# Cached-attention decode: one softmax per head, K scored beside the previous head's V, all loads through one ring

## The chip, the cores and the metric

The kernel runs on one core of a Trainium2 chip. The metric is the device time of one execution in microseconds; the medians below are of several executions of the same program. The runs of one round share a chip, but the rounds used three different chips, so runs of different rounds are compared by their ratio to the kernel before, which ran in every round. The engines are PE (TensorE matmul, with its weight loads, PEld, beside it), DVE (VectorE), ACT (ScalarE), POOL (GpSimd) and SP (SyncE, which here only issues DMA).

## The reference

One decode step: attention of one query over a cache of 65536 keys in each of 32 heads, a small SwiGLU feed-forward on the same input, and a gate that mixes both. K and V are 512 MiB each in bf16; everything else is about 14 MB. So 1087.64 MB must be read once, and nothing large is written.

```python
# x: [1, 1, 512]; k_cache, v_cache: [1, 32, 65536, 128]; all bf16
q = (x @ wq).reshape(1, 1, 32, 128).transpose(0, 2, 1, 3)
scores = einsum("bhqd,bhkd->bhqk", q, k_cache) * 128 ** -0.5
o = einsum("bhqk,bhkd->bhqd", softmax(scores), v_cache)
a = o.transpose(0, 2, 1, 3).reshape(1, 1, 4096) @ wo
b = (silu(x @ w_gate) * (x @ w_up)) @ w_down
g = sigmoid((x * gate_w).sum(-1, keepdims=True))
out = g * a + (1 - g) * b
```

## The kernel before

The keys are cut into 512 chunks of 4096 (16 per head), 32 blocks of 128 keys each. Of the 32 blocks of a chunk, 16 are transposed on PE and scored there; the other 16 are scored on DVE, by a product and a sum. Each chunk has its own softmax: the maximum over the chunk, which needs an all-reduce over the partitions, an exponential, and a sum. The chunks of a head are rescaled to a common maximum at the very end. The parts that matter, with cuts marked:

```python
# GpSimd: for every chunk, an all-reduce and then a scaling
for g in range(NGC):                                   # NGC = 512
    pool.wait_ge(s_mx, g + 1)
    nc.gpsimd.partition_all_reduce(amxt[:, g:g + 1], mxs[:, g % 4:g % 4 + 1],
                                   P, RMAX).then_inc(s_ar, 1)                    # L255
    pool.wait_ge(s_ar, g + 1)
    nc.gpsimd.tensor_scalar_mul(nbias[:, g % 4:g % 4 + 1], amxt[:, g:g + 1],
                                -SCALE).then_inc(s_nb, 1)                        # L258
# ScalarE
for i in range(NGC + 2):
    ...                                # half of the K^T copies, L277
    g = i - 2
    if g >= 0:
        act.wait_ge(s_nb, g + 1)
        nc.scalar.activation(pcol[:, g % 2, :], psS[:, g % SCORE_BANKS, 0:RB], ACT.Exp,
                             bias=nbias[:, g % 4:g % 4 + 1], scale=SCALE,
                             accum_out=rsum[:, g:g + 1]).then_inc(expdone, 1)    # L283
# VectorE
for c in range(NGC):
    ...                                # the other half of the K^T copies, L342
    g = c - 2
    if g >= 0:
        dve.wait_ge(qkdone, g + 1)
        dve.wait_ge(qkd, g + 2)
        nc.vector.reduce_max(mxs[:, g % 4:g % 4 + 1], psS[:, g % SCORE_BANKS, 0:RB], AX_X) # L348
    ...
    if c >= SCORE_BANKS:               # SCORE_BANKS = 3
        dve.wait_ge(expdone, c - SCORE_BANKS + 1)
    nc.vector.tensor_tensor(prod3, kblocks(c, TB, RB), qb3, ALU.mult)            # L366
    dve.wait_ge(s_tt, c + 1)
    nc.vector.reduce_sum(psS[:, c % SCORE_BANKS, TB:RB], prod3, AX_X)            # L368
# TensorE: scores (L468), transposes (L477) and value matmuls (L489) of one chunk each, in turn
```

Of the kernel before, what the change touches and what calls it, by code (L numbers as in the profile page):

```python
# [5 lines left out]
P = 128  # L6
CK = 4096
RB = CK // 128
TB = 16
TD = RB - TB  # L10
HTB = TB // 2
NS = 6
SCORE_BANKS = 3
PV_LAG = 3
PRODMODE = "bcast_f32"

ALU = mybir.AluOpType
ACT = mybir.ActivationFunctionType
BF16 = mybir.dt.bfloat16
# [6 lines left out]
def bass_gated_mix__mha_block_cached__swiglu_ffn__decode_kernel(  # L26
# [16 lines left out]
    assert Dh == 128 and D % 128 == 0 and F % 128 == 0 and S % (2 * CK) == 0  # L43
    Dc = D // 128
    FC = F // 128
    NCH = S // CK
    NGC = H * NCH
    NIT = NGC // 2
    SCALE = float(Dh) ** -0.5
    QT_COL0 = 64  # L50
    assert NGC <= 512

    with ExitStack() as ctx:
# [9 lines left out]
        psT = psum("psT", [P, 2 * TB, 128], BF16)  # L63
        psS = psum("psS", [P, SCORE_BANKS, 512], F32)
# [6 lines left out]
        bT = sb("bT", [P, 8], F32)  # L71
        gbc = sb("gbc", [P, 4], F32)
        sc = sb("scal", [P, 16], F32)
        qTb = sb("qTb", [P, max(H, 16)], BF16)
        xTb = sb("xTb", [P, 16], BF16)
        hbuf = sb("hbuf", [P, 3, 16], F32)
        guT = sb("guT", [P, 16], BF16)
        pcol = sb("pcol", [P, 2, RB], BF16)
        mxs = sb("mxs", [P, 4], F32)
        amxt = sb("amxt", [P, NGC], F32)  # L80
        nbias = sb("nbias", [P, 4], F32)
        rsum = sb("rsum", [P, max(NGC, D)], F32)
        Mt = sb("Mt", [P, max(H, 8)], F32)
        oh = sb("oh", [P, max(H, 8)], F32)
        lp = sb("lp", [P, max(H, 8)], F32)
        Lt = sb("Lt", [P, max(H, 8)], F32)
        oTn = sb("oTn", [P, max(H, 16)], BF16)
        finT = sb("finT", [P, 8], BF16)
        fin = sb("finrow", [P, 128], BF16)
        GQ = 4 if H % 4 == 0 else (2 if H % 2 == 0 else 1)  # L90
        NGQ = H // GQ
        diag = sb("diag", [P, 2, GQ * 128], BF16)
        ring = sb("ring", [P, NS, 2 * CK], BF16)

        s_x = sem("s_x")
        s_w1 = sem("s_w1")
        s_wq = sem("s_wq")
        s_wo = sem("s_wo")
        rs = [sem(f"rs{i}") for i in range(NS)]
        s_id0 = sem("s_id0")  # L100
        s_ident = sem("s_ident")
        s_ones = sem("s_ones")
        s_xT = sem("s_xT")
        s_xTb = sem("s_xTb")
        s_z = sem("s_z")
        s_e1 = sem("s_e1")
        s_dch = sem("s_dch")
        s_h = sem("s_h")
        s_sig = sem("s_sig")
        s_gu = sem("s_gu")  # L110
        s_q = sem("s_q")
        s_qTb = sem("s_qTb")
        s_b = sem("s_b")
        s_pro_dve = sem("s_pro_dve")
        s_diag = sem("s_diag")
        s_qbm = sem("s_qbm")
        s_qbc = sem("s_qbc")
        tdone = sem("tdone")
        qkdone = sem("qkdone")
        qkd = sem("qkd")  # L120
        ktd = sem("ktd")
        kta = sem("kta")
        pvdone = sem("pvdone")
        s_mx = sem("s_mx")
        s_ar = sem("s_ar")
        s_nb = sem("s_nb")
        expdone = sem("expdone")
        s_M = sem("s_M")
        s_ew = sem("s_ew")
        s_oh = sem("s_oh")  # L130
        s_L = sem("s_L")
        s_otn = sem("s_otn")
        s_a = sem("s_a")
        s_fin = sem("s_fin")
        s_tt = sem("s_tt")
        s_qrep = sem("s_qrep")
        s_gbc = sem("s_gbc")
        s_tr = sem("s_tr")
        s_fin2 = sem("s_fin2")
        s_out = sem("s_out")  # L140

        xr_dram = A_x.rearrange("a b d -> (a b) d")
        out_dram = out.rearrange("a b (c p) -> (a b c) p", p=P)
        gw_dram = gate_w.rearrange("(a d) -> a d", a=1)
        wq_dram = A_wq.rearrange("(c p) n -> p c n", p=P)

# [5 lines left out]
        VLAG = 1  # L152
        ring_order = []
        for j in range(NIT):
            ring_order.append(("k", j))
            if j >= VLAG:
                ring_order.append(("v", j - VLAG))
        for j in range(max(0, NIT - VLAG), NIT):
            ring_order.append(("v", j))
        slotK = {}  # L160
        fillK = {}
        slotV = {}
        fillV = {}
        for i, (kind, j) in enumerate(ring_order):
            if kind == "k":
                slotK[j] = i % NS
                fillK[j] = i // NS + 1
            else:
                slotV[j] = i % NS
                fillV[j] = i // NS + 1  # L170

        def kv_src(kind, j):
            h = (2 * j) // NCH
            cc = (2 * j) % NCH
            src = A_k_cache if kind == "k" else A_v_cache
            return src[0, h, cc * CK:(cc + 2) * CK, :].rearrange("(p r) d -> p (r d)", p=P)

        def kblock(c, r):
            slot = slotK[c // 2]
            rr = (c % 2) * RB + r  # L180
            return ring[:, slot, rr * 128:(rr + 1) * 128]

        def kblocks(c, r0, r1):
            slot = slotK[c // 2]
            rr0 = (c % 2) * RB + r0
            rr1 = (c % 2) * RB + r1
            return ring[:, slot, rr0 * 128:rr1 * 128].rearrange("p (a b) -> p a b", b=128)

        def vblock(c, r):
            slot = slotV[c // 2]  # L190
            rr = (c % 2) * RB + r
            return ring[:, slot, rr * 128:(rr + 1) * 128]

        dve_chain = [0]
        omg_cnt = [0]

        with ExitStack() as phaseW:
            base_w = nc.sbuf_base
            wq_t = phaseW.enter_context(nc.sbuf_tensor("wq_t", [P, Dc, H * Dh], BF16))
            wq_ap = wq_t[:]  # L200
            w_end = nc.sbuf_base
        with ExitStack() as phaseM:
            KT = phaseM.enter_context(nc.sbuf_tensor("KT", [P, 3 * TB, 128], BF16))
            qbc = phaseM.enter_context(nc.sbuf_tensor("qbc", [P, H, 128], BF16))
            prod = phaseM.enter_context(nc.sbuf_tensor("prod", [P, TD * 128],
                                                       BF16 if PRODMODE == "qrep_bf16" else F32))
            if PRODMODE == "qrep_bf16":
                qrep = phaseM.enter_context(nc.sbuf_tensor("qrep", [P, TD * 128], BF16))
            if nc.sbuf_base < w_end:
                padm = phaseM.enter_context(nc.sbuf_tensor("padm", [P, (w_end - nc.sbuf_base + 64) // 2], BF16))  # L210
            with ExitStack() as phaseA:
                wg_t = phaseA.enter_context(nc.sbuf_tensor("wg_t", [P, Dc, F], BF16))
                wu_t = phaseA.enter_context(nc.sbuf_tensor("wu_t", [P, Dc, F], BF16))
                wd_t = phaseA.enter_context(nc.sbuf_tensor("wd_t", [P, FC, D], BF16))
                wg_ap = wg_t[:]
                wu_ap = wu_t[:]
                wd_ap = wd_t[:]
                a_end = nc.sbuf_base
            phaseB = ExitStack()
            wo_t = phaseB.enter_context(nc.sbuf_tensor("wo_t", [P, H, D], BF16))  # L220
            wo_ap = wo_t[:]
            if nc.sbuf_base < a_end:
                padb = phaseB.enter_context(nc.sbuf_tensor("padb", [P, (a_end - nc.sbuf_base + 64) // 2], BF16))

            block = phaseB.enter_context(nc.Block())

            @block.sync
            def _(sp):
                sp.dma_start(xrow[0:1, :], xr_dram).then_inc(s_x, 16)
                sp.dma_start(gwrow[0:1, :], gw_dram).then_inc(s_x, 16)  # L230
                sp.dma_start(wq_ap, wq_dram).then_inc(s_wq, 16)
                sp.dma_start(wg_ap, wg_dram).then_inc(s_w1, 16)
                sp.dma_start(wu_ap, wu_dram).then_inc(s_w1, 16)
                sp.dma_start(wd_ap, wd_dram).then_inc(s_w1, 16)
                for i, (kind, j) in enumerate(ring_order):
                    slot = i % NS
                    if i >= NS:
                        pkind, pj = ring_order[i - NS]
                        if pkind == "k":
                            sp.wait_ge(tdone, 2 * pj + 2)  # L240
                            sp.wait_ge(qkd, 2 * pj + 2)
                        else:
                            sp.wait_ge(pvdone, 2 * pj + 2)
                    sp.dma_start(ring[:, slot, :], kv_src(kind, j)).then_inc(rs[slot], 16)

            @block.gpsimd
            def _(pool):
                nc.gpsimd.memset(ident[:], 0.0).then_inc(s_id0, 1)
                pool.wait_ge(s_id0, 1)
# [285 lines left out]
```

## Time and profile before

| | before |
|---|---|
| time, median of 3 | 7917.94 us |
| per chunk (span 7906.0 / 512) | 15.44 us |
| DMA over the span | 138 GB/s |
| busiest engine (DVE) | 34% |

No engine is full and DMA is far from it. The page's table of busy time, with three rows of the table of 40 slices below it (a digit is tenths; PEclk is the clock that the throttle granted to TensorE):

```profile
PE 1639.0 (21%) x33204; PEld 1500.1 (19%) x33205; DVE 2718.4 (34%) x2112; ACT 664.5 (8%) x1540; POOL 330.6 (4%) x1032
...
PEclk6555555555555555555555555555555555555555
DMA  6333333333333333333333333333333333333331
```

The DMA row above is the share of the 16 DMA engines' time. What limits a kernel like this is read from the chain of waits. One turn of it from mid-run (columns: start, duration, what):

```profile
4010.05 0.38 POOL amxt L255
4010.43 0.07 POOLq L258 x2
4010.50 6.99 issue
4017.49 0.27 POOL nbias L258
4017.76 0.02 issue
4017.78 0.39 ACT pcol L283 x2
4018.17 0.02 issue
4018.19 2.30 DVE prod L366
4020.50 0.02 issue
4020.52 2.29 DVE psS L368
```

All-reduce, 7 us of nothing, scaling, exponential, DVE product (it waits for the exponential of three chunks earlier, which frees its bank), DVE sum, maximum, next all-reduce: read as it stands, this is a loop in which nothing overlaps. A chain names the last releaser that the profile finds, and the all-reduce of a chunk does not wait for the maximum that stands in front of it here: by the semaphore count (`s_mx`, L255) it needs the maximum of its own chunk, which had ended 15.1 us earlier (median of the 512 chunks, counted in the trace).

```profile
57.37 0.18 DVE L348 TENSOR_REDUCE mxs<-psS 128x1 f32<-128x32 f32 x1
62.23 0.26 POOL L258 TENSOR_SCALAR nbias<-amxt 128x1 f32<-128x1 f32 x1 [7.45 <-issue]
...
69.84 0.38 POOL L255 PARTITION_ALL_REDUCE amxt<-mxs  x1 [7.35 <-issue]
...
L255 POOLq MODIFY_POOL_CONFIG  x1024: 1/11/11, 10.2 to 7877.9; - x171
```

The second maximum is ready at 57.55 us; its all-reduce starts at 69.84, 7.35 us after the scaling before it. Over the run 5.8 to 7.4 us lie between a scaling and the next all-reduce, 6.04 on average. So the loop is GpSimd's alone: all-reduce 0.38, 8.64 on average, scaling 0.26, 6.04 again, together 15.3 of the 15.44 us of a chunk. The DVE steps run beside it.

"issue" is time in which the engine waited for nothing that the profile shows. The two POOLq records in front of it are of the kind MODIFY_POOL_CONFIG; 1024 more are on the line of the all-reduce, two for each of its 512 calls. The all-reduce and the scaling alternate, and at every change from one to the other there is a pause: 6.04 us on average before an all-reduce and 8.64 us (6.7 to 10.6) before a scaling. The trace shows these records and the pause, and nothing of what goes on in it. For the scaling the table of waits sums the pauses (us in total, times, longest):

```profile
POOL nbias L258 <- issue: 4423.6, 512, 10.6
```

### The profile page before, as it was taken

The numbers are of one execution on the slowest core, as the hardware profiler recorded it, in microseconds if no ns is written. First come the engines' busy times: TensorE is split into PE (matmuls) and PEld (weight loads), VectorE is DVE, ScalarE is ACT, GpSimd is POOL, SyncE is SP. The second block draws the span as 40 slices with busy tenths as digits, with TensorE's granted clock in tenths as the row PEclk, the third lists the DMA queues.
The fourth block names the chain that finished last, engine by engine and source line by source line (L and its number), as shares of the span: only waits on it lengthen the run. The fifth ranks groups of instructions, "written<-read, shape, count | busy, mean of one in ns | idle before, by whom it ended". The sixth has DMA issues, their size and how long they took to land.

```text
span 7906.0 us, 74984 instructions
## 1 busy us (share of the span) xinstructions
PE 1639.0 (21%) x33204; PEld 1500.1 (19%) x33205; DVE 2718.4 (34%) x2112; ACT 664.5 (8%) x1540; POOL 330.6 (4%) x1032
## 2 busy tenths in 40 slices
PE   2222222221222222222222222122222222122221
PEld 2111111111111111111111111111111111111111
DVE  3333333333333333333333333333333333333332
ACT  0000000000000000000000000000000000000000
POOL 0000000000000000000000000000000000000000
PEclk6555555555555555555555555555555555555555
DMA  6333333333333333333333333333333333333331
GB/s 241 139 138 139 130 140 136 139 138 138 139 139 139 136 137 133 139 137 139 139 135 139 132 139 137 139 139 139 139 130 141 134 139 138 139 139 138 139 132 71
DMA packets 81569, 1092.46 MB, mean 138 GB/s; under 512 B 8282, under 2 KB 14172, under 8 KB 15196
## 3 DMA queue, kind: packets, MB, share of 16 engines
q1 hardware_dynamic: 77124, 1083.48, 37.2%
q8 instruction: 260, 4.26, 0.2%
q10 hardware_dynamic: 4120, 4.20, 0.2%
q14 instruction: 65, 0.53, 0.0%
HBM read 1087.64 MB, written 0.00 MB: 138 GB/s over the span
## 4 chain that ended last, share of the span: by engine, by line
issue 61%; DVE 31%; POOL 4%; ACT 2%; POOLq 1%; PE 0%; DMA 0%; DVEq 0%; another core or an unknown queue 0%; SPq 0%
DVE prod L366 15%; DVE psS L368 15%; POOL amxt L255 2%; ACT pcol L283 2%; POOL nbias L258 2%; DVE mxs L348 1%; POOLq L258 0%; DVE KT L342 0%; DMA wq_t<-in_A_wq_dram 0%; DVE diag L318 0%; DVEq L360 0%; DVE qbc L323 0%; PE psS L500 0%; PE psS L421 0%; POOLq L506 0%
## 5 line engine op out<-in xcount | busy, mean ns | idle before, releaser
L366 DVE TENSOR_TENSOR prod<-ring,qbc 128x2048 f32<-128x2048 bf16 x512 | 1173.7, 2292 | 5095.7 <-ACT pcol L283 5095.7
L489 PE MATMUL psO<-pcol,ring 128*128 128x1 bf16 x16384 | 518.6, 166 | 6224.3 <-ACT pcol L283 6224.3
L489 PEld LDWEIGHTS psO<-pcol,ring 128*128 128x128 bf16 x16384 | 476.7, 104 | 6358.8 <-ACT pcol L283 6358.8
L368 DVE TENSOR_REDUCE psS<-prod 128x16 f32<-128x2048 f32 x512 | 1175.0, 2295 | 17.4
L477 PE MATMUL psT<-ident,ring 128*128 128x128 bf16 x8192 | 955.8, 311 | 0.0
L477 PEld LDWEIGHTS psT<-ident,ring 128*128 128x128 bf16 x8192 | 831.6, 145 | 0.0
L283 ACT ACTIVATE pcol<-psS,nbias 128x32 bf16<-128x32 f32 x512 | 147.3, 288 | 7182.8 <-POOL nbias L258 7182.8
L277 ACT ACTIVATE KT<-psT 128x1024 bf16<-128x1024 bf16 x512 | 519.2, 1014 | 9.9 <-PE psT L477 9.9
L342 DVE COPY KT<-psT 128x1024 bf16<-128x1024 bf16 x512 | 348.4, 681 | 1.6 <-PE psT L477 1.6
L255 POOL PARTITION_ALL_REDUCE amxt<-mxs x512 | 195.6, 382 | 3128.5 <-DVE mxs L348 3067.4
L258 POOL TENSOR_SCALAR nbias<-amxt 128x1 f32<-128x1 f32 x512 | 133.7, 261 | 4423.6 <-issue 4423.6
L468 PE MATMUL psS<-qTb,KT 128*128 128x1 bf16 x8192 | 289.3, 165 | 6.5 <-DVE psS L368 6.5
L468 PEld LDWEIGHTS psS<-qTb,KT 128*128 128x128 bf16 x8192 | 258.0, 104 | 7.1 <-DVE psS L368 7.1
L283 ACT ACTIVATION_READ_ACCUMULATOR pcol<-psS,nbias 128x1 f32 x512 | 98.7, 193 | 0.0
L348 DVE TENSOR_REDUCE mxs<-psS 128x1 f32<-128x32 f32 x510 | 91.9, 180 | 0.0
L382 DVE TENSOR_REDUCE Mt<-amxt 128x32 f32<-128x512 f32 x1 | 0.7, 686 | 25.9 <-POOL nbias L258 25.9
L318 DVE TENSOR_SCALAR diag<-ident,psS 128x128 bf16<-128x128 bf16 x32 | 6.0, 252 | 0.0
L421 PE MATMUL psS<-xTb,wq_t 128*128 128x1 bf16 x128 | 3.5, 165 | 11.5 <-DMA wq_t<-in_A_wq_dram 11.5
L421 PEld LDWEIGHTS psS<-xTb,wq_t 128*128 128x128 bf16 x128 | 3.5, 104 | 11.6 <-issue 11.6
L311 DVE CAST qTb<-psS 128x32 bf16<-128x32 f32 x1 | 0.2, 192 | 14.6 <-PE psS L421 14.6
L500 PE MATMUL psS<-oTn,wo_t 128*128 128x1 bf16 x128 | 3.6, 165 | 6.9 <-DVE oTn L398 6.9
L500 PEld LDWEIGHTS psS<-oTn,wo_t 128*128 128x128 bf16 x128 | 3.5, 104 | 7.0 <-DVE oTn L398 7.0
(51 smaller groups left out, 37.4 us busy)
## 6 DMA issues: line engine op xcount, KB each, us to landing
ring<-in_A_k_cache_dram SPq DMA_DIRECT2D x256, 2048.0 KB, 7.7
ring<-in_A_v_cache_dram SPq DMA_DIRECT2D x256, 2048.0 KB, 7.7
wq_t<-in_A_wq_dram SPq DMA_DIRECT2D x1, 4096.0 KB, 12.6
wo_t<-in_A_wo_dram ACTq DMA_DIRECT2D x1, 4096.0 KB, 40.8
wg_t<-in_B_w_gate_dram SPq DMA_DIRECT2D x1, 1792.0 KB, 16.8
wu_t<-in_B_w_up_dram SPq DMA_DIRECT2D x1, 1792.0 KB, 21.7
wd_t<-in_B_w_down_dram SPq DMA_DIRECT2D x1, 1792.0 KB, 26.4
xrow<-in_A_x_dram SPq DMA_DIRECT2D x1, 1.0 KB
```

What stands on the lines that cost most here:

```text
L255: nc.gpsimd.partition_all_reduce(amxt[:, g:g + 1], mxs[:, g % 4:g % 4 + 1], P, RMAX).then_inc(s_ar, 1)
L258: nc.gpsimd.tensor_scalar_mul(nbias[:, g % 4:g % 4 + 1], amxt[:, g:g + 1], -SCALE).then_inc(s_nb, 1)
L277: nc.scalar.activation(KT[:, (i % 3) * TB + HTB:(i % 3) * TB + TB, :], psT[:, pair * TB + HTB:pair * TB + TB, :], ACT.Copy, bias=0.0).then ...
L283: nc.scalar.activation(pcol[:, g % 2, :], psS[:, g % SCORE_BANKS, 0:RB], ACT.Exp, bias=nbias[:, g % 4:g % 4 + 1], scale=SCALE, accum_out=r ...
L342: nc.vector.tensor_copy(KT[:, (c % 3) * TB:(c % 3) * TB + HTB, :], psT[:, pair * TB:pair * TB + HTB, :]).then_inc(ktd, 1)
L348: nc.vector.reduce_max(mxs[:, g % 4:g % 4 + 1], psS[:, g % SCORE_BANKS, 0:RB], AX_X).then_inc(s_mx, 1)
L366: nc.vector.tensor_tensor(prod3, kblocks(c, TB, RB), qb3, ALU.mult).then_inc(s_tt, 1)
L368: nc.vector.reduce_sum(psS[:, c % SCORE_BANKS, TB:RB], prod3, AX_X).then_inc(qkd, 1)
L468: last = nc.tensor.matmul(psS[:, bank, k:k + 1], KT[:, (cq % 3) * TB + k, :], qTb[:, hq:hq + 1], start=True, stop=True)
L477: last = nc.tensor.transpose(psT[:, pair * TB + k, :], kblock(c, k), ident[:])
L489: last = nc.tensor.matmul(psO[:, cp:cp + 1], vblock(cp, k), pcol[:, cp % 2, k:k + 1], start=(k == 0), stop=(k == RB - 1))
L500: last = nc.tensor.matmul(psS[:, 0, cb:cb + 1], wo_ap[:, h, cb * 128:(cb + 1) * 128], oTn[:, h:h + 1], start=(h == 0), stop=(h == H - 1))
```

## The change

The intent: one softmax per head in place of 16, so that its latency hides behind the scoring of the next head; all K on TensorE, so that DVE only copies and takes maxima; and all loads, weights too, through one ring of nine 2 MB slots. The work is cut into 2048 groups of 8 blocks. PE repeats a step of 8 transposes of group g, 8 value matmuls of group g - 76 (a head has 64 groups, so this is the previous head) and 8 scores of group g - 2. The core of the diff, heavily cut:

```diff
-NS = 6
-SCORE_BANKS = 3
-PV_LAG = 3
+GB = 8
+NSLOT = 9
+NPT = 5
+NKT = 6
+LAG_QK = 2
+LAG_PV = 12
@@ GpSimd
-                for g in range(NGC):
-                    pool.wait_ge(s_mx, g + 1)
-                    nc.gpsimd.partition_all_reduce(amxt[:, g:g + 1], mxs[:, g % 4:g % 4 + 1], ...
-                    nc.gpsimd.tensor_scalar_mul(nbias[:, g % 4:g % 4 + 1], amxt[:, g:g + 1], ...
+            for h in range(H):
+                w("s_mx", h + 1)
+                nc.gpsimd.partition_all_reduce(amx[:, h:h + 1], mxs[:, h:h + 1], P, RMAX)...
+                w("s_ar", h + 1)
+                nc.gpsimd.tensor_scalar_mul(nbias[:, h:h + 1], amx[:, h:h + 1], -SCALE)...
@@ ScalarE: odd groups
+            for g in range(1, NG, 2):
+                h, r = divmod(g, GPH)
+                if r == 9 and h >= 1:
+                    softmax(h - 1)          # waits for s_nb; exponential of 128 x 512 scores
+                w("tdone", g + 1)
+                nc.scalar.activation(KT[:, g % NKT, :], kt_ps(g), ACT.Copy, bias=0.0)...
@@ VectorE: even groups
-                        nc.vector.tensor_tensor(prod3, kblocks(c, TB, RB), qb3, ALU.mult)...
-                    nc.vector.reduce_sum(psS[:, c % SCORE_BANKS, TB:RB], prod3, AX_X)...
+                if r == 4 and h >= 1:
+                    top(h - 1)              # maximum of the previous head
+                nc.vector.tensor_copy(KT[:, g % NKT, :], kt_ps(g))...
@@ TensorE
+            for g in range(n_steps):
+                if g < NG:
+                    transposes(g)
+                if 0 <= g - first_pv < NG:
+                    values(g - first_pv)    # first_pv = GPH + LAG_PV = 76
+                if 0 <= g - LAG_QK < NG:
+                    scores(g - LAG_QK)
+                if g == mid:
+                    out_proj(...)           # of the first 31 heads
```

## The prediction

> **What bounds the kernel now.** One serial loop per 4096-key chunk. The span is 7906 us for 512 chunks, 15.44 us each. The chain of waits in mid-run repeats: all-reduce of the maximum on GpSimd 0.38 us, then "issue" 7.0 or 10.2 us, scalar multiply 0.27, exponential on ScalarE 0.39, DVE product 2.30, DVE reduction 2.29, the rest of the K copy 0.45, maximum 0.19, then the next all-reduce. The table of waits puts 4423.6 us of "issue" before the 512 multiplies: 8.64 us per chunk, over half the period. In the trace two MODIFY_POOL_CONFIG records stand there. [...]this trace shows 6 us before each all-reduce and 7 to 10 before each multiply. Nothing is full: the busy table has PE 21%, DVE 34%, and DMA moves 138 GB/s.
>
> **What the change does.**
> - Removed: 480 of 512 all-reduce/reload rounds, all 512 DVE products and reductions (2349 us busy), the rescaling at the end.
> - Added on PE: all 16384 K blocks are transposed and scored there instead of 8192. From the timeline: 16 transposes take 1.87 us with a 0.31 us drain, so 104 ns each; scores and value matmuls run at 27 ns each (32 in 0.85 us, 16 in 0.42). The prologue's transposes at full granted clock also take 105 ns, so a warm clock will not help.
> - Copies of K^T: 1024 on DVE at 0.68 us (697 us), 1024 on ScalarE at 1.01 us (1039 us). Neither fills up.
> - Moved: a head's reduction and exponential run beside the next head's scoring; values lag 12 groups.
>
> **New limits (estimates from these durations).**
> - PE: a step of 8 blocks is 8x(104+27+27) = 1.26 us; 2048 steps = 2589 us. Before it, wq and the q projection take about 18 us; FFN 9, output projection and end about 20. Sum about 2635.
> - DMA: with the ring loading freely and no small-row weights (30 to 39.5 us) the stretch table shows 433 GB/s; 10 to 60 us gives 413. 1092 MB at those: 2520 to 2645 us.[...]
> So PE is the limit by a hair, with DMA within some per cent.
> - Per head: maximum (~0.7), all-reduce (0.4), reload 7 to 10, multiply, exponential (~0.9) follow the last score; ScalarE waits for it before its group 9. Against the 8 or so steps available I expect a PE stall of 0 to 2.5 us per head, about 35 us in all.
> - [...]
>
> **Prediction: 2690 us, 8 in 10 between 2620 and 2820; faster by over 2%: 0.99, within: 0.005, slower: 0.005.** A speedup of about 2.94.
>
> **What would show it.** PE and its weight loads nearly continuous in mid-run; a steady step of about 1.26 us; transposes still ~104 ns; DMA about 405 GB/s, its share above 0.9; SyncE waiting mainly for freed slots (transposes and values done); GpSimd waiting ~70 us per head for the maximum; DVE about 28% busy, ScalarE 42%; once per head a hole of up to 2.5 us on PE after ScalarE's wait for the scaled maximum. If DMA bounds instead, PE waits at ring loads.
>
> **What would make it wrong.** Sustained DMA under 400 GB/s[...] (2750 to 2850); a bubble when PE turns from transposes to value matmuls, a transition the old trace never shows without a wait (0.1 us is 200 us in all); reloads over 10 us under full DMA; instruction fetch falling behind; or transposes that speed up[...] (below 2620).

The sum comes to 2690 us: about 2635 for PE, 35 for the holes and 20 in one more term. That term, a guess that no measured number backs, and other passages that no trace or run here shows are cut where marked. "Reload", here and in the expectations, is the word for the pause between the two kinds of GpSimd call, and no more than the pause was measured. "Warm" stands for a full granted clock, "cold" for half of it.

## The result

The changed kernel takes 2721.9 us (median of 4, 2714.97 to 2738.49) against 7916.53 us before. The ratio is 0.344 (95% interval 0.3429 to 0.3451). Ratios here are the mean time of one kernel's fast runs over that of the other's of the same rounds, so they are not quite the ratio of the medians quoted. The prediction of 2690 (2620 to 2820) holds it.

The page of the changed kernel, the same rows:

```profile
PE 2569.2 (94%) x49442; PEld 2554.8 (93%) x49442; DVE 731.8 (27%) x1073; ACT 1068.3 (39%) x1091; POOL 21.8 (1%) x71
...
PEclk8755556555565555555556655555555555555555
DMA  9999999999999999999999999999999999999997
...
DMA packets 81695, 1094.32 MB, mean 400 GB/s; under 512 B 8307, under 2 KB 14198, under 8 KB 15222
```

Two things are full at once, PE at 94% and the DMA share at nine tenths and above, and the page alone does not say which of them sets the pace. (The share alone is no ceiling: this page has 400 GB/s at 97.1% for the ring's queue, that of e3_wide32, further down, 416 GB/s at 98.3%.) PE's clock is granted at half speed nearly everywhere (mean 0.539). The timeline of one step in mid-run (start, duration, engine, line, operation):

```profile
1331.13 0.77 PEld L352 LDWEIGHTS psT<-ident,ring 128*128 128x128 bf16 x8
1331.16 1.01 PE L352 MATMUL psT<-ident,ring 128*128 128x128 bf16 x8
1331.86 0.42 PEld L383 LDWEIGHTS psO<-pcol,ring 128*128 128x128 bf16 x8
1332.20 0.29 PEld L366 LDWEIGHTS psS<-qTb,KT 128*128 128x128 bf16 x8
1332.41 0.77 PEld L352 LDWEIGHTS psT<-ident,ring 128*128 128x128 bf16 x8
```

From 1331.13 to 1332.41 is one step: 1.28 us, where 1.26 was predicted. 2048 of them are 2621 us. But in the first head, while the clock is granted in full, a pair of transposes and scores repeats faster:

```profile
72.33 0.46 PEld L352 LDWEIGHTS psT<-ident,ring 128*128 128x128 bf16 x8
72.35 0.61 PE L352 MATMUL psT<-ident,ring 128*128 128x128 bf16 x8
72.74 0.31 PEld L366 LDWEIGHTS psS<-qTb,KT 128*128 128x128 bf16 x8
72.97 0.45 PEld L352 LDWEIGHTS psT<-ident,ring 128*128 128x128 bf16 x8
```

0.64 us here, in a stretch with PEclk at 1.00 from 51.81 to 103.01 us; at half clock the same pair took 1.06 to 1.07 us (at 40.94 and 42.01 us). From 47.1 to 51.8 us, just before the clock went to 1.00, PE ran transposes and one-column scores alone. Eight transposes span 0.61 us in place of 1.01, so one takes about 55 ns in place of 107. The prediction had said that a full clock would not help. It had read 105 ns from the prologue of the kernel before, where the table of stretches says that the clock is full:

```profile
30.00:40.00 10.00, 6.28 (x176) 5.43 (x177) 3.93 (x16) 0.18 (x1) 0.00 (x0) 1.00 0.99 421
```

That is a stretch of 10 us of the kernel before: its busy times by engine, then the clock 1.00, the DMA share and GB/s. The timeline of the same kernel has there:

```profile
39.41 3.57 PE L477 MATMUL psT<-ident,ring 128*128 128x128 bf16 x32
```

32 transposes in 3.57 us, with a last one of about 0.31, is (3.57 - 0.31) / 31 = 105 ns at "1.00". In the changed kernel, too, the first transposes (21.99 us) stand in a stretch shown as 1.00 and take 1.01 us for eight. In the packed trace its first throttle record comes at 24.50 us, and from 24.94 us on eight transposes take 0.61 us; in the kernel before the first record comes at 43.73 us, after those transposes. So in both runs transposes at the 1.00 ahead of the first throttle record took the 105 to 107 ns of half clock, and not the 55 ns of the 1.00 after it; the author reads that first 1.00 as a default and not a measurement. Later repetitions of the kernel before fit this but do not show it: some have a clock of 1.0 for the whole run, others 0.503, at the same time (7910.95 and 7915.17 us), but PE, busy for 21%, does not limit that kernel.

Last, the hole per head. ScalarE stands before its group 9 until the scaled maximum arrives, and PE soon needs that group (timeline, head 16):

```profile
1347.71 0.38 POOL L213 PARTITION_ALL_REDUCE amx<-mxs  x1 [73.61 <-DVE mxs L288]
...
1358.29 0.26 POOL L215 TENSOR_SCALAR nbias<-amx 128x1 f32<-128x1 f32 x1 [10.20 <-issue]
1358.59 0.69 ACT L229 ACTIVATE pcol<-psS,nbias 128x512 bf16<-128x512 f32 x1 [4.88 <-POOL nbias L215]
...
1360.34 0.37 PE L366 MATMUL psS<-qTb,KT 128*128 128x1 bf16 x8 [2.38 <-ACT KT L244]
```

The pause stands between all-reduce and scaling as before, 10.2 us here, and PE is idle 2.38 us. The table of waits sums it:

```profile
POOL nbias L215 <- issue: 342.1, 32, 12.7
...
PE psS L366 <- ACT KT L244: 96.5, 32, 4.9
```

So the questions are: what sets the pace, PE or DMA; why the clock stays at half for an engine that is 94% busy; what the holes cost; and how much of the gain was due to the restructuring at all.

### The profile page after: what moved, and what is told of

Its sections match the earlier page's. It is cut to its first block, busy times and chain, and to the rows that moved or that the text cites. A ratio compares the mean times of both kernels' runs of the same rounds, so it can differ in the third digit from the quotient of the medians.

```text
span 2736.7 us, 103879 instructions
## 1 busy us (share of the span) xinstructions
PE 2569.2 (94%) x49442; PEld 2554.8 (93%) x49442; DVE 731.8 (27%) x1073; ACT 1068.3 (39%) x1091; POOL 21.8 (1%) x71
## 3 DMA queue, kind: packets, MB, share of 16 engines
q1 hardware_dynamic: 81270, 1087.67, 97.1%
## 4 chain that ended last, share of the span: by engine, by line
PE 80%; issue 14%; DVE 2%; DMA 2%; ACT 1%; POOL 1%; SPq 1%; POOLq 0%; ACTq 0%
PE psT L352 54%; PE psS L366 14%; PE psO L383 12%; ACT KT L244 1%; DMA ring<-in_A_k_cache_dram 1%; DVE KT L307 1%; DVE mxs L288 1%; DMA ring<-in_A_v_cache_dram 1%; SPq L198 1%; POOL amx L213 0%; PE psT L411 0%; POOL nbias L215 0%; ACT pcol L229 0%; PE psT L383 0%; PE psO L404 0%
## 5 line engine op out<-in xcount | busy, mean ns | idle before, releaser
L352 PE MATMUL psT<-ident,ring 128*128 128x128 bf16 x16384 | 1999.8, 300 | 20.2 <-DMA ring<-in_A_k_cache_dram 14.8
L244 ACT ACTIVATE KT<-psT 128x1024 bf16<-128x1024 bf16 x1024 | 1044.9, 1024 | 1451.9 <-PE psT L352 1451.9
L352 PEld LDWEIGHTS psT<-ident,ring 128*128 128x128 bf16 x16384 | 1518.8, 135 | 20.9 <-DMA ring<-in_A_k_cache_dram 13.6
L307 DVE COPY KT<-psT 128x1024 bf16<-128x1024 bf16 x1024 | 708.4, 692 | 1943.1 <-PE psT L352 1943.1
L366 PE MATMUL psS<-qTb,KT 128*128 128x1 bf16 x16384 | 720.6, 165 | 107.8 <-ACT KT L244 96.5
L383 PEld LDWEIGHTS psO<-pcol,ring 128*128 128x128 bf16 x15872 | 811.6, 115 | 7.3 <-issue 7.3
L383 PE MATMUL psO<-pcol,ring 128*128 128x1 bf16 x15872 | 782.0, 170 | 6.0 <-issue 6.0
L366 PEld LDWEIGHTS psS<-qTb,KT 128*128 128x128 bf16 x16384 | 594.9, 103 | 111.8 <-ACT KT L244 100.4
L229 ACT ACTIVATE pcol<-psS,nbias 128x512 bf16<-128x512 f32 x32 | 22.0, 687 | 181.0 <-POOL nbias L215 181.0
L213 POOL PARTITION_ALL_REDUCE amx<-mxs x32 | 12.2, 382 | 2329.8 <-DVE mxs L288 2329.8
L215 POOL TENSOR_SCALAR nbias<-amx 128x1 f32<-128x1 f32 x32 | 8.4, 261 | 342.1 <-issue 342.1
L229 ACT ACTIVATION_READ_ACCUMULATOR pcol<-psS,nbias 128x1 f32 x32 | 6.2, 193 | 0.0
```

What stands on the lines that cost most here:

```text
L213: nc.gpsimd.partition_all_reduce(amx[:, h:h + 1], mxs[:, h:h + 1], P, RMAX).then_inc(sm["s_ar"], 1)
L215: nc.gpsimd.tensor_scalar_mul(nbias[:, h:h + 1], amx[:, h:h + 1], -SCALE).then_inc(sm["s_nb"], 1)
L229: nc.scalar.activation(pcol[:, h % 2, :], psS[:, h % 2, 0:NC_H], ACT.Exp, bias=nbias[:, h:h + 1], scale=SCALE, accum_out=rsum[:, h:h + 1]) ...
L244: nc.scalar.activation(KT[:, g % NKT, :], kt_ps(g), ACT.Copy, bias=0.0).then_inc(sm["ev_a"], 1)
L307: nc.vector.tensor_copy(KT[:, g % NKT, :], kt_ps(g)).then_inc(sm["ev_d"], 1)
L352: last = nc.tensor.transpose(dst[:, k * 128:(k + 1) * 128], src[:, b * 128:(b + 1) * 128], ident[:])
```

## The experiments

Theory P: PE at half clock sets the pace, with the holes on top. Rival D: DMA is at its ceiling. Theory C, a guess that the runs are to test: the clock stays at half because the array streams columns for too small a part of the time. Scores and value matmuls stream one column each; from the 107 ns of a transpose's 128 columns at half clock a step streams 8 x 107 ns = 0.86 us of 1.28, 67% (an estimate from these durations, as are all streamed shares below). Where V was loaded in part the comparison with the reference passed all the same, so that a pass says nothing about those.

| run | time, us (median) | ratio to before | mean clock, profiled run |
|---|---|---|---|
| changed kernel | 2721.9 | 0.344 | 0.539 |
| e0_before_act: before, scaling on ScalarE | 2727.98 | 0.3447 | 0.509 |
| e1_act: changed, scaling on ScalarE | 2664.91 | 0.3367 | 0.522 |
| e3_wide32: changed, 32-column scores | 2635.11 | 0.3329 | 0.841 |
| e6_wide16: changed, 16-column scores | 2635.63 | 0.3328 | 0.791 |
| e4_both: e1 and e3 together | 2635.42 | 0.3329 | 0.839 |
| e2_halfv: changed, half V (wrong) | 2708.6 | 0.3422 | 0.545 |
| e8_both_halfv: e4, half V (wrong) | 2262.0 | 0.2861 | 0.916 |
| e9_few_halfv: changed, few value matmuls, half V (wrong) | 2026.38 | 0.2559 | 0.883 |
| e12_both_eighthv: e4, an eighth of V (wrong) | 2212.76 | 0.2793 | 0.916 |
| e11_both_again: e4 once more | 2634.72 | 0.3325 | 0.837 |
| e10_best: e4, projection earlier | 2626.07 | 0.3314 | 0.839 |

### e0_before_act: one line of the kernel before

```diff
@@ GpSimd
-                    pool.wait_ge(s_ar, g + 1)
-                    nc.gpsimd.tensor_scalar_mul(nbias[:, g % 4:g % 4 + 1], amxt[:, g:g + 1],
-                                                -SCALE).then_inc(s_nb, 1)
@@ ScalarE
-                        act.wait_ge(s_nb, g + 1)
+                        act.wait_ge(s_ar, g + 1)
+                        nc.scalar.activation(nbias[:, g % 4:g % 4 + 1], amxt[:, g:g + 1], ACT.Copy, bias=0.0,
+                                             scale=-SCALE).then_inc(s_nb, 1)
+                        act.wait_ge(s_nb, g + 1)
```

> The kernel before, with only the scaling of the maximum moved from GpSimd to ScalarE[...]. Theory (most of the gain of the change is the removal of the reloads, not the restructuring): the 8.6 us of issue per chunk vanish, ScalarE adds about 0.3 us; 15.44 - 8.64 + 0.3 is about 7.1 us for each of 512 chunks, 3500 to 3750 us in all, correct results. Rival (the 7 to 10 us belong to the all-reduce itself, whatever follows it): the time stays near 7900 us.

2727.98 us, correct: the time of the changed kernel within 0.3%. With one kind of call left on GpSimd the MODIFY_POOL_CONFIG records of the all-reduce's line fall from 1024 to 2, and the theory holds more strongly than it was stated. The expected 7.1 us per chunk was too much, because it took away only the 8.64 us before the scaling and kept the rest as serial. The 6.04 us before the all-reduce go too, and the DVE work had been running beside them all along. It is what is left: the softmax of a chunk finishes within the three banks' slack, and DVE runs without a gap (page):

```profile
PE 1721.1 (63%) x33205; PEld 1539.8 (56%) x33205; DVE 2670.9 (98%) x2112; ACT 767.3 (28%) x2052; POOL 1183.6 (43%) x520
...
L255 POOL PARTITION_ALL_REDUCE amxt<-mxs x512 | 1182.2, 2309 | 1521.7 <-DVE mxs L348 1518.2
```

The chain of waits is DVE at 90%, with the maxima of two chunks 5.22 us apart (1304.10 and 1309.32 us). The all-reduce itself now shows 2.31 us where it showed 0.38 us before; it falls together with the DVE product. It has the time.

### e1_act: the changed kernel without the pauses

```diff
@@ GpSimd
-                w("s_ar", h + 1)
-                nc.gpsimd.tensor_scalar_mul(nbias[:, h:h + 1], amx[:, h:h + 1], -SCALE).then_inc(sm["s_nb"], 1)
@@ ScalarE, in softmax(h)
+                w("s_ar", h + 1)
+                nc.scalar.activation(nbias[:, h:h + 1], amx[:, h:h + 1], ACT.Copy, bias=0.0,
+                                     scale=-SCALE).then_inc(sm["s_nb"], 1)
                 w("s_nb", h + 1)
```

> The changed kernel with the same single move: no reload in the softmax of a head. Theory P (TensorE sets the pace): the hole of about 3 us per head, 108 us in all, disappears and comes off the time nearly whole: 2610 to 2650 us, PE waits for ScalarE near 0. Rival D (DMA is at its ceiling, its share being 97%): the hole is only where PE waits for data anyway, the time stays within 20 us of 2722. A third possibility: without the hole TensorE never gets its stretches of full clock and gives part of the gain back.

2664.91 us: 57 us less, so D, which allowed 20, falls. P alone, at 2610 to 2650, does not quite hold; the third possibility does. The holes are gone (PE's wait for ScalarE's copies has left the head of the table of waits) and PE is busy without interruption, but the clock no longer leaves one half after the first head. The table of stretches, three of 1000, 1000 and 400 us:

```profile
200.00:1200.00 1000.00, 1000.00 (x18750) 1000.00 (x18749) 277.65 (x403) 409.89 (x427) 4.20 (x12) 0.50 1.00 414
1200.00:2200.00 1000.00, 999.36 (x18742) 999.28 (x18741) 276.97 (x402) 409.78 (x427) 4.21 (x12) 0.50 1.00 412
2200.00:2600.00 400.00, 400.00 (x7496) 400.00 (x7495) 110.91 (x161) 164.57 (x172) 1.75 (x5) 0.50 1.00 412
```

PE is busy 1000.00 of 1000.00 us and is granted half its clock throughout. In the changed kernel the same three stretches have 0.54, 0.53 and 0.50: eight of its holes are followed within about 10 us by full clock, nine stretches of 10 to 20 us in which PE catches up. One of them, and the 20 us after it:

```profile
780.00:799.00 19.00, 16.96 (x473) 16.79 (x471) 6.92 (x10) 10.10 (x10) 0.00 (x0) 1.00 0.98 398
800.00:820.00 20.00, 19.80 (x371) 19.54 (x370) 5.54 (x8) 7.37 (x8) 0.00 (x0) 0.50 1.01 427
...
798.47 0.20 PE L366 MATMUL psS<-qTb,KT 128*128 128x1 bf16 x2 [1.35 <-issue]
```

All nine end within 2.2 us of such a gap of 1.0 to 2.2 us in which PE waits for nothing that the profile shows (what these gaps are is read off under e12_both_eighthv). Gaps of up to 1.16 us in the first head (at 76.73, 89.39 and 95.86 us) did not end its full clock. So the holes cost 96.5 us and gave a part of it back as full clock; the 57 us are what was left to gain. Across the four runs of the changed kernel time and clock go together: 2738.49 us at 0.539, 2723.95 at 0.549, 2719.86 at 0.554, 2714.97 at 0.559.

### e3_wide32 and e6_wide16: more columns per score

```diff
-        qTb = sb("qTb", [P, max(H, 16)], BF16)
+        qTb = sb("qTb", [P, H + 32], BF16)            # columns from H on set to 0
@@ scores(g)
-                    last = mm(psS[:, h % 2, col:col + 1], KT[:, g % NKT, k * 128:(k + 1) * 128],
-                              qTb[:, h:h + 1], start=True, stop=True)
+                    n = min(32, NC_H - col)
+                    last = mm(psS[:, h % 2, col:col + n], KT[:, g % NKT, k * 128:(k + 1) * 128],
+                              qTb[:, h:h + n], start=True, stop=True)
```

A score now writes its own column and 31 (or 15) more, which the following scores overwrite in order; the result is correct.

> The changed kernel with score matmuls that stream 32 columns in place of 1 (31 of them garbage, overwritten by the next blocks; result still correct). At half clock 32 columns take 27 ns, [...]so the step should stay 1.28 us if the clock does not change. Theory C (the clock stays at half because the array streams only 0.85 of 1.28 us per step): streaming rises to 83%, the clock is granted as in the first head, transposes fall from 107 to 55 ns, and DMA becomes the limit: 2550 to 2620 us, mean clock over 0.75. Rival (the clock has nothing to do with streamed columns): mean clock near 0.54, 2700 to 2740 us. Rival D (DMA bound now): time unchanged even if the clock rises.

The 27 ns are an estimate (107 ns x 32 / 128), and 27 ns is also what the prediction read for a one-column score.

2635.11 us at a mean clock of 0.841. The time lies just above the expected 2550 to 2620, the clock as expected, and both rivals fall: the clock follows the added columns, and D, which wanted no change of time, is refuted for the changed kernel. The rows of the page, and the head of its chain of waits:

```profile
PEclk8988888888888888888888888788888887888886
...
DMA 53%; PE 29%; issue 14%; DVE 1%; ACT 1%; POOL 1%; SPq 1%; POOLq 0%; ACTq 0%
```

PE now waits for K loads (283.3 us in 164 waits) where it had waited 14.8 us. In the version with both moves PE waits 4.24 us for a K load up to 1313.64 us, and eight transposes then take 1.04 us, the time of half clock (PEclk is 0.65 on average from 1310 to 1315 us, 1.00 in the 5 us before). The step there is 1.29 us (between the transposes' weight loads at 1313.64 and 1314.93 us), against 1.28 with one column: the 31 extra columns cost no time even at half clock.

> The changed kernel with scores that stream 16 columns (correct result): by the durations of the trace a cold step then streams 0.85 + 8 x 0.013 = 0.96 of 1.28 us, 75%, between the 67% that stay at half clock and the 80 to 83% that get the full one. Theory C with a threshold below 75%: like 32 columns, 2630 to 2640 us and mean clock above 0.8. With a threshold above 75%: like one column, about 2720 us and mean clock near 0.55.[...]

2635.63 us, mean clock 0.791 (just under the expected 0.8): like 32 columns. So steps of 67% ran at a mean clock of 0.522 (e1_act) and 0.539, steps of 75% at 0.791; what brings the clock up between them was not shown. And in the full-clock stretches of the changed kernel a step takes 0.85 us (783.48 to 784.33 us) and streams 8 x 55 ns = 0.44 us of it, 52%, and yet the clock there stays at 1.00 until a gap (799.33 us).

### e2_halfv: fewer bytes for the changed kernel

```diff
+                dst, src = view(job), source(job)
+                if job[0] == "v" and i >= 4 * NSLOT:
+                    dst, src = dst[:, 0:SLOT // 2], src[:, 0:SLOT // 2]
-                sp.dma_start(view(job), source(job)).then_inc(ld[i % NSLOT], 16)
+                sp.dma_start(dst, src).then_inc(ld[i % NSLOT], 16)
```

(This one starts after four rounds of the ring.)

> The changed kernel, loading only the first half of each V slot (the rest of the slot keeps older data; result wrong on purpose), so that DMA moves about 25% less. Theory P (TensorE at half clock sets the pace): 2600 to 2730 us, PE step 1.28 us, DMA near 310 GB/s. Rival D (DMA sets the pace): the time follows the bytes, 2000 to 2150 us.

2708.6 us with 837 MB in place of 1094 MB, at 308 GB/s. A quarter of the bytes is worth half a per cent, within the noise of the two ratios (0.3408 to 0.3436 here, 0.3429 to 0.3451 for the changed kernel). P holds and D is dead for the changed kernel.

### e4_both, e8_both_halfv: does DMA limit the version with wide scores?

e4_both joins the edits of e1_act and e3_wide32; e8_both_halfv adds the edit of e2_halfv.

> Both moves. If theories P and C hold: TensorE has slack at full clock, DMA alone limits, no hole per head: 2540 to 2600 us, little better than wide scores alone (which can catch up after each hole). If C falls and P holds: as the move to ScalarE alone, 2610 to 2650. If D holds: 2700 to 2740.

2635.42 us, no better than the 2635.11 of wide scores alone, where PE still waited 106.3 us for ScalarE's copies: with the clock at 0.84 PE catches up, and the holes cost nothing. It is 35 us above the expected range; DMA moves 419 to 422 GB/s in mid-run and not the 433 of the short stretch that the prediction had read. The chain of waits:

```profile
DMA 80%; PE 18%; issue 1%; SPq 1%; ACT 0%; DVE 0%; ACTq 0%
```

> Wide scores and no reload, with the same halved V loads (result wrong on purpose). If DMA is what limits that version at 2635 us, the time follows the bytes: 1960 to 2080 us. If something else limits it (PE, or waits on slots), it stays above 2400 us.

2262 us: lower by 373 us (by the ratios of the two rounds 0.2861 against 0.3329), so DMA limits e4_both, but above the 1960 to 2080 expected, and nothing in the expectation covers it. PE limits again (84% of the chain), with gaps in the middle of groups of matmuls:

```profile
1315.40 0.33 PE L373 MATMUL psS<-qTb,KT 128*128 128x32 bf16 x7 [1.62 <-issue]
```

Between this gap and the one before it (at 1309.19 us) stand exactly 128 matmuls, which with their weight loads are 256 instructions. The table of waits has 119.9 + 116.9 + 57.5 = 294 us of them. The page of this run counts the packets of queue 8, whose kind is "instruction" (packets, MB, share):

```profile
q8 instruction: 386, 6.32, 1.0%
```

386 packets of 16 KiB for 98884 matmuls and weight loads is one for every 256, the spacing of the two gaps; e9_few_halfv below has 278 for 71170, again one for 256.

### e12_both_eighthv: are the gaps instruction loads that stand behind full DMA queues?

The edit of e8_both_halfv with an eighth of each V slot.

> Wide scores, no reload, V loads cut to one eighth (result wrong on purpose), so that DMA needs about 56% of the time of the full loads and its queues must run empty between loads. The version with half V stayed at 2262 us with 310 us of PE gaps of 1.5 to 3.5 us that fall 128 matmuls apart (256 instructions with the weight loads), with PE waiting for nothing that the profile shows. Theory F (those gaps are instruction fetch, slow because its loads stand behind full DMA queues): gaps fall below 120 us, time 1830 to 2000 us. Rival (fetch is slow whatever DMA does, or the gaps are something else): gaps stay near 300 us and the time above 2150 us.

2212.76 us with 112.9 + 90.2 + 45.9 = 249 us of gaps (the half-V run had 294 by its table, not the 310 of the expectation) at a DMA share of 78%, again about 128 matmuls apart, or a multiple of that. The kept traces settle the first half of theory F: all 250 such gaps over 0.15 us in e8_both_halfv (past the first 60 us) and all 224 here end 1.2 to 1.6 us after a packet of queue 8 has landed, while only 9% of all matmuls start 1.1 to 1.7 us after one. That PE waits in these gaps for its instructions is the author's reading of it; no record says so. In the changed kernel, which is at half clock for most of its time, gaps in which PE waits for nothing sum to 27 us (11.2 + 6.0 + 5.2 + 4.6), and those over 0.15 us (past the first 60 us) end 1.1 to 1.6 us after such a packet, too. The second half falls, as far as this run goes: with the share of the ring's queue down from 93.5 to 77.6%, though not to a queue that is mostly empty, only 45 us of them go away. Why the versions with a mean clock of 0.916 have so much more of these gaps stays open. The gaps do not bear on e4_both, where DMA sets the pace and PE's waits for nothing sum to about 50 us.

### e9_few_halfv: a larger streamed share without wide scores

```diff
                     col = rh * GB + k
+                    if h < H - 1 and not (col == 0 or k == GB - 1):
+                        continue
                     last = mm(acc, ...
```

with the halved V loads of e2_halfv; scores have one column.

> The changed kernel with narrow scores, with only one of eight value matmuls left and V loads halved (result wrong on purpose). Raises the streamed share without widening anything: a cold step is 8 x (107 + 27) = 1.07 us plus one value matmul, 78% streamed, as in the first head, which got the full clock. Theory C: the clock rises, PE is no limit, DMA is: 1960 to 2080 us, mean clock above 0.7. Rival (it was the width of the score matmuls, not the share): clock 0.5 to 0.55, PE sets the pace at about 1.1 us a step, 2230 to 2350 us.

2026.38 us, mean clock 0.883 (0.89 and 0.90 in mid-run), DMA 412 GB/s: as theory C wants, and the width of the scores is not needed. It also shows that loads of half slots still move 417 GB/s in mid-run, so e8_both_halfv was indeed not held up by DMA.

### e10_best and e11_both_again: the end of the kernel

In e4_both PE starts on the last V slot at 2619.09 us; 8.24 us of output projection then run before the last 56 value matmuls, because the projection is placed after the first group of that last slot.

```diff
-            mid = NG + first_pv - GPC
+            mid = NG + first_pv - 4 * GPC
```

> Wide scores, no reload, and the output projection of the first 31 heads moved from the last V slot to three slots earlier, where PE waits about 3 us for each V load. In the version without this move the last V slot lands 12 us before the end, and 8.2 us of that are the projection. If the end of the kernel is that chain: 6 to 8 us less than the control of the same call (2627 to 2630 against 2635). Rival (DMA finishes later for another reason): no difference.

> Control for the earlier projection: wide scores and no reload once more, 2633 to 2638 us as before.

2626.07 against 2634.72 us in the same rounds, 8.6 us less, a little more than the expected 6 to 8: the projection now runs in the waits for V. This is the best version: ratio 0.3314 to before (95% interval 0.3309 to 0.3319), 3.5% below the changed kernel by the medians, and correct.

## Why the prediction was right, and where it was not

- **What bounded the kernel before: right in what it named, wrong in the loop.** The pause between all-reduce and scaling was named, and the 6 us before each all-reduce too. But the prediction laid the DVE steps end to end with them in one serial loop, where GpSimd alone takes 15.3 of the 15.44 us. So it did not see that the pauses were all that mattered: e0_before_act takes them away by themselves and reaches 2727.98 us. The 2349 us of DVE work that the change removes were listed as a part of the gain, but all of DVE's work together is 2718 us busy, and once it overlaps it takes no longer than PE takes in the changed kernel. The change exchanges one full engine for another of nearly the same length.
- **PE is the limit, DMA within some per cent: right.** e2_halfv (a quarter of the bytes, 0.5% of the time) and e3_wide32 (2635 us as soon as PE is faster) show both halves.
- **The step: a term slightly mis-sized.** 1.28 us in place of 1.26; over 2048 steps 33 us.
- **The holes: mis-sized.** "About 35 us in all" took pauses of 7 to 10 us; in the changed kernel, with DMA at 97.1%, they took 8 to 12.7 us, 342.1 / 32 = 10.7 on average, and PE waited 96.5 us. The prediction listed "reloads over 10 us under full DMA" as what could go wrong.
- **"A warm clock will not help": wrong.** This is the step about the new kernel that failed. Transposes take 55 ns at full clock and 107 at half. The figure of 105 ns at 1.00 came from a stretch before the first throttle record (43.73 us). The error did little harm to the total only because the changed kernel spends nearly all its time at half clock (mean 0.539). A prediction built on a PE at full clock would have expected DMA to bind: 0.85 us a step, read in the full-clock stretches, is 1741 us for 2048 steps (an estimate), and DMA was put at 2520 to 2645.
- **What cancelled.** The prediction's 2690 plus 33 for the steps and 62 for the holes (96.5 - 35) is 2785, more than the 2737 of the profiled run. The stretches of full clock, in the first head and after some holes, go the other way. That they make up the 48 us is an estimate by difference. A count in the trace bears it out: 59.4 groups in the 51.2 us of the first head take 12 us less than at the 1.07 us of half clock, and 128.6 groups in the 129.7 us of the nine later stretches 35 us less than at 1.28, 47 us together. e1_act shows only that without holes these stretches vanish, and that removing 96.5 us of holes gains 57 us.
- **Signs named in advance.** DMA 400 GB/s (405 predicted), DVE 27% (28), ScalarE 39% (42), GpSimd 72.8 us per head waiting for the maximum (2329.8 / 32; 70 predicted), SyncE waiting mainly for value matmuls (2376.7 us).

Open: why a hole of 2 to 5 us is sometimes (8 of 32), and not always, followed by full clock; why the gaps that end after an instruction packet sum to 294 and 249 us at a mean clock of 0.916 and to 27 us at 0.539; and whether the clock goes with the share of streamed columns itself or with something beside it: tried were only 67% (mean clock 0.522 and 0.539) and 75% and more (0.791 and up), and stretches at 52% kept a clock of 1.00 that had come before.

## What to carry to other kernels

Before restructuring, take away the one wait that the chain names and run that (and count the semaphores: a step of the chain may be a coincidence in time): here moving one tiny scaling to another engine gave the whole 2.9x (7911.97 to 2727.98 us), and the large rewrite added nothing until its own new limits were found. When an engine at 94% and DMA at 97% compete, cut one side's work on purpose and see which the time follows. And judge the TensorE clock by the durations of its matmuls: in e1_act PE, with transposes and one-column matmuls, was busy 1000.00 of 1000.00 us at a clock of 0.50, and in e3_wide32 31 columns that nobody needs took the mean clock to 0.841 and the time down to 2635.11 us.
